# Clamps of converted weights on VectorE in place of GpSimd, and their rounding on ScalarE, in a kernel of attention and two MLPs

## The chip, the cores and the metric

The kernel runs on one core of a Trainium2 chip. A core has five engines that run their own instruction streams side by side: TensorE (PE in the profile, and PEld for its weight loads), VectorE (DVE), ScalarE (ACT), GpSimd (POOL) and SyncE (SP, which here only issues DMAs). The metric is the time of one execution on the device in microseconds, lower is better.

## The reference, cut to what matters

```python
# attention (per batch and head; s = 576 tokens, m = 32 memory rows, d = 64)
a = phi - np.max(phi, axis=2, keepdims=True); a = np.exp(a)
a = a / (np.sum(a, axis=2, keepdims=True) + 1e-09)
k_m = np.einsum('bhsm,bhsd->bhmd', a, k)
v_m = np.einsum('bhsm,bhsd->bhmd', a, v)
scores = scale * np.matmul(q, k_m.transpose(0, 1, 3, 2))
scores = scores - np.max(scores, axis=-1, keepdims=True)
attn = np.exp(scores); attn = attn / (np.sum(attn, axis=-1, keepdims=True) + 1e-09)
x = np.matmul(attn, v_m)            # laid out as 2304 tokens x 512
# first MLP, w_in 512 x 2048, w_out 2048 x 512
h = x @ w_in
x = (h * (1.0 / (1.0 + np.exp(-1.702 * h)))) @ w_out
# norm and second MLP, w_gate and w_val 512 x 1536, w_out 1536 x 512
xn = x / np.sqrt(np.mean(x * x, axis=-1, keepdims=True) + 1e-06) * rms_g
g = xn @ w_gate
out = (g * (1.0 / (1.0 + np.exp(-g))) * (xn @ w_val)) @ w_out
```

The attention's inputs are float32. The five weight matrices come as float64 and are turned into float32 on the chip, by operations on their bits.

## The kernel before, in words

Every float32 product is taken as three passes over TensorE: each operand is split into a high part h (rounded to TensorE's fast 32-bit form) and a low part l, and x y is h h' + l h' + h l'. So each operand of TensorE needs a rounding (h) and a subtraction (l = x - h).

**Staging.** The four batches are worked on as two pairs. For each batch and half of its heads (a unit) the kernel loads k, v, q and phi, takes the softmax of phi, k_m and v_m, and the scores and their softmax. attn @ v_m @ w_in is taken as attn @ (v_m @ w_in), so that v_m @ w_in (vm_part, L422) is a weight of the first MLP. The first MLP runs over 8 blocks of 256 hidden units: a_g1 (L454, then GELU L460 on ScalarE, rounding L462 on ScalarE, low part L109 on GpSimd into gr) and a_g2 (L483), whose results VectorE adds from PSUM into x2 (L491, here called the eviction). a_g2's results go through three PSUM buffers. While pair 0 passes its first MLP, the attention of pair 1 runs beside it as side work. Then pair 1 passes its first MLP, with the RMS norm of pair 0 beside it; the norm of pair 1 (norm_1 to norm_4, L504 to L553) comes in the transition to the second MLP: squares on ScalarE, their sums on GpSimd (L508, L510, low part L109), column sums on TensorE (L521), root and reciprocal (L528, VectorE), transposes (L535). The second MLP (b_g3 at L577, b_g4 at L608) runs over 6 blocks of 256 hidden units.

**The weights' conversion** (w_load and w_conv, from L127). A piece is 128 rows of 512 float64 numbers, 512 KB. It is loaded into one of three raw buffers by SyncE (L133, L135). Then, on the bits: ScalarE takes the absolute value of the upper words into one of three cv buffers (L152); L153 clamps it to the range that float32 holds; VectorE shifts it (L157) and merges in the sign (L161) and the lower word's bits (L164). Pieces of the first MLP are also written to a cache in DRAM from ScalarE's DMA queue (L168), and the second pair loads them from there as float32. At last the high part is rounded by copy(to_h, ...) (L102 where it runs on GpSimd, L106 where on ScalarE) and the low part subtracted (L109, on GpSimd but for one piece). There are 68 conversions: 32 pieces of the first MLP and 36 of the second.

**What sets the order.** A table written by hand gives the first steps, about the first 100 us, and names the engine of some steps; run() gives the rest by rule: after each a_g1 or b_g3 come the conversions due at this place, a load for two pieces ahead, side work, and the a_g2 or b_g4 of the step before. A second table gives the transition. The framework's scheduler then orders each engine's stream by its own estimate of times; an engine executes its stream strictly in this order, and a waiting instruction holds all behind it.

Of the kernel before, what the change touches and what calls it, by code (L numbers as in the profile page):

```python
# [18 lines left out]
def kernel(  # L19
# [43 lines left out]
    MINW = 2.0**-15  # bits 0x38000000  # L63
    MAXW = 122872.0  # bits 0x47EFFC00
# [77 lines left out]
    def w_conv(hf, clamp=G, to_h=G, to_l=G):  # L142
        """float64 to float32, on the bits: sign and top exponent bit, then the other exponent
        bits and the fraction 3 to the left. What is out of float32's range is clamped."""
        raw = loaded.pop(hf)
        if hf[:2] == ("a", 1):
            t = raw[:, :512]
        else:
            bits = raw.rearrange("p (n t) -> p n t", t=2)
            lo, hi = bits[:, :, 0], bits[:, :, 1]  # L150
            t = cvp.tile([P, 512], U32, tag="cv", name="cv")
            nc.scalar.activation(out=t.bitcast(F32), in_=hi.bitcast(F32), func=AF.Abs)  # L152
            clamp.tensor_scalar(  # L153
                out=t.bitcast(F32), in0=t.bitcast(F32), scalar1=MINW, scalar2=MAXW,
                op0=ALU.max, op1=ALU.min,
            )
# [21 lines left out]
    # A unit is four heads of a batch. Where its k and v lay, q^T and the softmax of its scores follow.  # L178
    # The four 32-row blocks of an odd batch hold heads 2, 3, 0, 1.
# [164 lines left out]
    def soft(u, hp):  # L344
        """Of a unit's softmax, blocks 2 hp and 2 hp + 1, by parity and chunk pair; and its sums."""
# [79 lines left out]
        # An odd batch's heads 2, 3, 0, 1 lie in its blocks, so the rows' halves  # L425
        # are of different batches.
# [244 lines left out]
    # Side work of each pass, in the order of its issue.  # L671
# [40 lines left out]
    # Batch 0 first: its share of the first MLP runs beside the rest of batch 1's attention.  # L712
    for s in (
# [24 lines left out]
        (w_conv, w2[1], G, G, V), (a_g1, 0, 1, 1), (w_load, w2[3]), (a_g1, 0, 1, 2),  # L738
# [25 lines left out]
    # The norm of the second pair runs beside the second MLP of the first.  # L764
# [52 lines left out]
```

## Time and profile before

| what | value |
| --- | --- |
| time, median of 3 runs | 922.22 us (921.48 to 923.67) |
| profiled execution, span from first to last instruction | 919.6 us |
| TensorE busy | 866.3 us, 94% |
| VectorE busy | 556.7 us, 61% |
| GpSimd busy | 496.5 us, 54% |
| ScalarE busy | 382.2 us, 42% |

The trace is of one execution, and its only time is the span; the runs of the first line are others. Attention of both pairs and the first MLP of pair 0 last until about 260 us, the first MLP of pair 1 follows until about 440, the transition until about 500, and then the second MLP. The shares are averages over these stages; the rows below take them apart.

### The profile page before, as it was taken

The numbers are of one execution on the slowest core, as the hardware profiler recorded it, in microseconds if no ns is written. First come the engines' busy times: TensorE is split into PE (matmuls) and PEld (weight loads), VectorE is DVE, ScalarE is ACT, GpSimd is POOL, SyncE is SP. The second block draws the span as 40 slices with busy tenths as digits, with TensorE's granted clock in tenths as the row PEclk, the third lists the DMA queues.
The fourth block names the chain that finished last, engine by engine and source line by source line (L and its number), as shares of the span: only waits on it lengthen the run. The fifth ranks groups of instructions, "written<-read, shape, count | busy, mean of one in ns | idle before, by whom it ended". The sixth has DMA issues, their size and how long they took to land.

```text
span 919.6 us, 14798 instructions
## 1 busy us (share of the span) xinstructions
PE 866.3 (94%) x5702; PEld 823.1 (90%) x5702; DVE 556.7 (61%) x997; ACT 382.2 (42%) x823; POOL 496.5 (54%) x450
## 2 busy tenths in 40 slices
PE   3887997997999999999998999999999999999997
PEld 2776997986999999999988999999999999999997
DVE  5699896788965456558778155366348328333333
ACT  2366773654667765554466342122122122111110
POOL 2377998897987695979994162064046018001000
PEclk9989998999999999999999999999999999999999
DMA  9974559433221120223313021012004001000123
GB/s 215 258 218 124 165 137 244 160 118 108 90 70 46 48 69 25 69 73 101 92 47 92 1 92 46 1 46 92 0 1 124 14 1 47 1 1 1 46 58 103
DMA packets 40534, 74.62 MB, mean 81 GB/s; under 512 B 3856, under 2 KB 16144, under 8 KB 40464
## 3 DMA queue, kind: packets, MB, share of 16 engines
q1 hardware_dynamic: 35856, 65.29, 26.2%
q10 hardware_dynamic: 4608, 8.39, 2.6%
q8 instruction: 45, 0.74, 0.3%
q14 instruction: 25, 0.20, 0.1%
HBM read 60.56 MB, written 13.11 MB: 80 GB/s over the span
## 4 chain that ended last, share of the span: by engine, by line
PE 72%; POOL 8%; DVE 7%; DMA 6%; issue 4%; SPq 2%; ACT 1%; ACTq 0%; POOLq 0%; DVEq 0%
PE pg L577 31%; PE pg L608 16%; PE pg L483 14%; PE pg L454 7%; POOL cv L153 2%; DMA stage<-in_k_dram 2%; DVE cv L161 2%; PE pvm L422 2%; DMA raw_a_out<-in_moe_w_out_dram 2%; POOL gr L109 2%; DVE cv L164 1%; DVE x L491 1%; DMA stage<-in_v_dram 1%; DVE cv L157 1%; DMA raw_a_in<-in_moe_w_in_dram 1%
## 5 line engine op out<-in xcount | busy, mean ns | idle before, releaser
L483 PE MATMUL pg<-gr,a_outh 128*128 128x288 f32 x1024 | 231.4, 301 | 11.7 <-DVE x L491 10.2
L483 PEld LDWEIGHTS pg<-gr,a_outh 128*128 128x128 f32 x1024 | 172.8, 190 | 16.4 <-DVE x L491 14.7
L483 PE MATMUL pg<-gr,a_outl 128*128 128x288 f32 x512 | 151.6, 297 | 0.0
L153 POOL TENSOR_SCALAR cv<-cv 128x512 f32<-128x512 f32 x67 | 137.1, 2051 | 22.8 <-ACT cv L152 20.8
L608 PE MATMUL pg<-b_o2h,pp 128*128 128x512 f32 x432 | 139.7, 391 | 0.0
L586 DVE TENSOR_TENSOR pf<-sg,pg 128x384 f32<-128x384 f32 x72 | 39.6, 552 | 158.2 <-PE pg L577 151.0
L109 POOL TENSOR_TENSOR gr<-gf,gr 128x288 fp32r<-128x288 f32 x128 | 115.9, 920 | 34.8 <-ACT gr L462 30.1
L491 DVE TENSOR_TENSOR x<-x,pg 128x288 f32<-128x288 f32 x224 | 95.9, 446 | 61.8 <-PE pg L483 60.7
L102 POOL TENSOR_SCALAR b_o2h<-cv 128x512 fp32r<-128x512 f32 x12 | 8.4, 716 | 223.6 <-PE pg L577 223.4
L584 ACT ACTIVATE sg<-pg 128x384 f32<-128x384 f32 x72 | 35.4, 492 | 159.1 <-PE pg L577 159.0
L483 PEld LDWEIGHTS pg<-gr,a_outl 128*128 128x128 f32 x512 | 97.1, 190 | 0.0
L608 PEld LDWEIGHTS pg<-b_o2h,pp 128*128 128x128 f32 x432 | 81.1, 188 | 16.1
L588 ACT CAST pp<-pf 128x384 fp32r<-128x384 f32 x72 | 37.0, 513 | 126.9 <-DVE pf L586 126.6
L608 PE MATMUL pg<-b_o2l,pp 128*128 128x512 f32 x216 | 84.8, 393 | 0.0
L616 DVE TENSOR_TENSOR oacc<-oacc,pg 128x512 f32<-128x512 f32 x90 | 61.1, 683 | 24.1 <-PE pg L608 24.1
L460 ACT ACTIVATE gf<-pg 128x288 f32<-128x288 f32 x128 | 51.6, 410 | 53.4 <-POOL gr L109 25.2
L109 DVE TENSOR_TENSOR pp<-pf,pp 128x384 fp32r<-128x384 f32 x72 | 46.3, 643 | 34.9 <-ACT pp L588 34.9
L462 ACT CAST gr<-gf 128x288 fp32r<-128x288 f32 x128 | 53.5, 432 | 28.8 <-PE pg L483 25.3
L577 PE MATMUL pg<-xnh,b_gateh 128*128 128x384 f32 x288 | 62.6, 337 | 0.0
L577 PE MATMUL pg<-xnh,b_vall 128*128 128x384 f32 x288 | 62.3, 337 | 0.0
L577 PE MATMUL pg<-xnh,b_gatel 128*128 128x384 f32 x288 | 62.3, 336 | 0.0
L157 DVE TENSOR_SCALAR cv<-cv 128x512 uint32<-128x512 uint32 x68 | 52.0, 765 | 17.0 <-POOL cv L153 16.9
(183 smaller groups left out, 1849.4 us busy)
## 6 DMA issues: line engine op xcount, KB each, us to landing
raw_a_in<-in_moe_w_in_dram SPq DMA_DIRECT2D x16, 512.0 KB, 4.2
raw_a_out<-in_moe_w_out_dram SPq DMA_DIRECT2D x16, 512.0 KB, 4.3
cache<-cv ACTq DMA_DIRECT2D x32, 256.0 KB, 3.8
raw_b_gate<-in_moe_w_gate_dram SPq DMA_DIRECT2D x12, 512.0 KB, 3.7
raw_b_val<-in_moe_w_val_dram SPq DMA_DIRECT2D x12, 512.0 KB, 3.8
raw_b_o<-in_moe_w_out_dram SPq DMA_DIRECT2D x12, 512.0 KB, 3.6
stage<-in_k_dram SPq DMA_DIRECT2D x8, 576.0 KB, 12.1
stage<-in_v_dram SPq DMA_DIRECT2D x8, 576.0 KB, 11.6
```

Source lines behind the costliest of these rows:

```text
L109: eng.tensor_tensor(out=lo, in0=full, in1=hi.bitcast(F32), op=ALU.subtract)
L153: clamp.tensor_scalar(out=t.bitcast(F32), in0=t.bitcast(F32), scalar1=MINW, scalar2=MAXW, op0=ALU.max, op1=ALU.min,)
L157: nc.vector.tensor_scalar(out=t, in0=t, scalar1=3, scalar2=0x3FFFFFFF, op0=ALU.logical_shift_left, op1=ALU.bitwise_and,)
L454: nc.tensor.matmul(ps[:, :HALF], lhsT=a[:, b, c, f], rhs=at[:, y, c, n], start=(i == 0), stop=(i == 5),)
L460: nc.scalar.activation(out=gf[:, :HALF], in_=ps[:, :HALF], func=AF.Gelu_apprx_sigmoid)
L462: nc.scalar.copy(out=gr[:, 0, :HALF], in_=gf[:, :HALF])
L483: nc.tensor.matmul(ps[:, :HALF], lhsT=wo[a][:, fc, es], rhs=gr[fc][:, y, :HALF], start=(i == 0), stop=(i == 5),)
L491: nc.vector.tensor_tensor(out=acc[:, e, n], in0=acc[:, e, n], in1=ps[:, :HALF], op=ALU.add)
L577: nc.tensor.matmul(ps[:, :TB], lhsT=w[a][:, e, f], rhs=xs[y][:, e, n], start=(i == 0), stop=(i == 3 * NE - 1),)
L586: nc.vector.tensor_tensor(out=pf, in0=sg, in1=pss[1][:, :TB], op=ALU.mult)
L608: nc.tensor.matmul(ps, lhsT=pp[fc][:, a, ks], rhs=w[y][:, fc], start=(i == 0), stop=(i == 5))
L616: nc.vector.tensor_tensor(out=o, in0=o, in1=ps, op=ALU.add)
```

## The change

The clamp (L153) of every converted piece is issued on VectorE. Before, one of the 68 ran there and 67 on GpSimd. The rounding of the high part of every converted piece is issued on ScalarE; before, 6 of these ran there and 62 on GpSimd. GpSimd keeps the rounding of pieces that the second pair loads from the cache, and the low parts. Comments are emptied too; the line numbers stay. The diff's core, with three of the six changed lines of the table:

```diff
-    def w_conv(hf, clamp=G, to_h=G, to_l=G):
+    def w_conv(hf, to_h=None, to_l=G):
...
             nc.scalar.activation(out=t.bitcast(F32), in_=hi.bitcast(F32), func=AF.Abs)
-            clamp.tensor_scalar(
+            nc.vector.tensor_scalar(
                 out=t.bitcast(F32), in0=t.bitcast(F32), scalar1=MINW, scalar2=MAXW,
                 op0=ALU.max, op1=ALU.min,
             )
...
         x, (h, l) = t.bitcast(F32), wt[key]
-        copy(to_h, h[:, c], x)
+        copy(to_h or (G if hf[:2] == ("a", 1) else A), h[:, c], x)
         sub_lo(to_l, l[:, c], x, h[:, c])
...
-        (att_k5, b0), (att_k5, b1), (w_load, w0[3]), (w_conv, w0[1], G, A), (vm_part, 0, 0, 0),
+        (att_k5, b0), (att_k5, b1), (w_load, w0[3]), (w_conv, w0[1]), (vm_part, 0, 0, 0),
...
-        (w_conv, w1[1], G, A), (w_conv, w2[0], V, A), (a_g2, 0, 0, 0), (aside,),
+        (w_conv, w1[1]), (w_conv, w2[0]), (a_g2, 0, 0, 0), (aside,),
...
-        (w_conv, w2[1], G, G, V), (a_g1, 0, 1, 1), (w_load, w2[3]), (a_g1, 0, 1, 2),
+        (w_conv, w2[1], A, V), (a_g1, 0, 1, 1), (w_load, w2[3]), (a_g1, 0, 1, 2),
```

The scheduler orders the streams anew. Three places follow. Numbers behind a name tell instances apart (cv_2153 is one piece's conversion, gr_1879 one GELU's parts), and what stands in brackets is what the instruction waits for.

On ScalarE, before, where the attention of the third unit (kmisc2_1) runs beside the first MLP's fourth block; gf and gr are GELU and its rounding:

```order
L462 CAST gr_1790<-gf_1788 128x288 [waits PE_49,Activation_49]
L168 DMA cache_102<-cv_1969 128x512 [waits DMAHW5_49,DVE_49]
L460 ACTIVATE gf_1865<-pg1_1858 128x288 [waits Pool_49]
L462 CAST gr_1867<-gf_1865 128x288 [waits PE_49,Activation_49]
L245 ACT_TABLE_LOAD [waits DMAHW7_49]
L245 ACTIVATE kmisc2_1_1440<-kmisc2_1_1440 96x768 [waits Pool_49]
L460 ACT_TABLE_LOAD
L460 ACTIVATE gf_1877<-pg1_1870 128x288 [waits Pool_49]
L462 CAST gr_1879<-gf_1877 128x288 [waits PE_49,Activation_49]
```

The cache write of cv_1969 waits for DMA semaphore 5; the roundings gr_1867 and gr_1879 follow with no Abs between them.

On ScalarE, after, the same cache write, and then the stretch up to gr_1879:

```order
L168 DMA cache_102<-cv_1969 128x512 [waits DMAHW4_49,DVE_49]
L460 ACTIVATE gf_1865<-pg1_1858 128x288 [waits Pool_49]
L106 CAST a_0_4_outh_1976<-cv_1969 128x512
L242 COPY kmisc2_1_1440<-pk3_1616 96x128 [waits PE_49]
L168 DMA cache_102<-cv_2074 128x512 [waits DMAHW6_49,DVE_49]
L460 ACTIVATE gf_1877<-pg1_1870 128x288 [waits Pool_49]
L106 CAST a_0_4_outh_1976<-cv_2074 128x512
```

```order
L462 CAST gr_1867<-gf_1865 128x288 [waits PE_49,Activation_49]
L460 ACT_TABLE_LOAD
L460 ACTIVATE gf_1952<-pg1_1945 128x288 [waits Pool_49]
L460 ACTIVATE gf_1964<-pg1_1957 128x288 [waits Pool_49]
L152 ACTIVATE cv_2153<-raw_a_0_5_in_0_1980 128x512 [waits DMAHW3_49,DMAHW2_49]
L297 ACTIVATE kz_1720<-pk4_1689,rv_1716 128x64 [waits DVE_49,PE_49]
L302 ACTIVATE vz_1724<-pk4_1689,rv_1716 128x64 x2
L462 CAST gr_1879<-gf_1877 128x288 [waits PE_49]
L433 CAST vm0_4h_1982<-pvm_1984 64x2x256 [waits PE_49]
```

The write of cv_1969 waits for DMA semaphore 4 now, roundings of weights (L106) have come between the GELUs, and the Abs of cv_2153 has moved up, ahead of gr_1879. That Abs waits for its piece's load.

On VectorE, before, the evictions of the same block (pg2):

```order
L491 TENSOR_TENSOR x2_0_822<-x2_0_822,pg2_1753 128x288
L491 TENSOR_TENSOR x2_0_822<-x2_0_822,pg2_1761 128x288
L491 TENSOR_TENSOR x2_0_822<-x2_0_822,pg2_1826 128x288
L491 TENSOR_TENSOR x2_0_822<-x2_0_822,pg2_1834 128x288
L491 TENSOR_TENSOR x2_0_822<-x2_0_822,pg2_1842 128x288
L251 TENSOR_REDUCE kmisc2_1_1440<-kmisc2_1_1440 96x128
L491 TENSOR_TENSOR x2_0_822<-x2_0_822,pg2_1850 128x288
```

On VectorE, after, from pg2_1826 on:

```order
L491 TENSOR_TENSOR x2_0_822<-x2_0_822,pg2_1826 128x288
L491 TENSOR_TENSOR x2_0_822<-x2_0_822,pg2_1834 128x288
L287 TENSOR_SCALAR rv_1716<-pk4s_1714 128x1
L290 RECIPROCAL rv_1716<-rv_1716 128x1
L291 TENSOR_SCALAR rv_1716<-maskeo_99,rv_1716 128x3
L491 TENSOR_TENSOR x2_0_822<-x2_0_822,pg2_1842 128x288
L153 TENSOR_SCALAR cv_2153<-cv_2153 128x512
L491 TENSOR_TENSOR x2_0_822<-x2_0_822,pg2_1850 128x288
L157 TENSOR_SCALAR cv_2153<-cv_2153 128x512
L161 SCALAR_TENSOR_TENSOR cv_2153<-raw_a_0_5_in_0_1980,cv_2153 128x512
```

Here too cv_2153 has moved up: its clamp and its shift stand on either side of pg2_1850.

On GpSimd, before, in the transition, the norm of pair 1 (sq and sr are squares and their sums) and pieces of the second MLP's second block (b_1):

```order
L508 TENSOR_TENSOR sq0_1_0_5895<-sq0_1_0_5895,sq1_1_0_5896 128x768
L153 TENSOR_SCALAR cv_6341<-cv_6341 128x512
L510 TENSOR_TENSOR sq0_1_0_5895<-sq0_1_0_5895 128x384
L109 TENSOR_TENSOR sr_5901<-sq0_1_0_5895,sr_5901 128x384
L508 TENSOR_TENSOR sq0_1_1_6004<-sq0_1_1_6004,sq1_1_1_6005 128x768
L102 TENSOR_SCALAR b_1_gateh_6019<-cv_6013 128x512
L102 TENSOR_SCALAR b_1_gateh_6019<-cv_6267 128x512
L510 TENSOR_TENSOR sq0_1_1_6004<-sq0_1_1_6004 128x384
L109 TENSOR_TENSOR b_1_gatel_6020<-cv_6013,b_1_gateh_6019 128x512
L109 TENSOR_TENSOR b_1_gatel_6020<-cv_6267,b_1_gateh_6019 128x512
L153 TENSOR_SCALAR cv_6535<-cv_6535 128x512
L109 TENSOR_TENSOR sr_6010<-sq0_1_1_6004,sr_6010 128x384
```

On GpSimd, after, the same place:

```order
L508 TENSOR_TENSOR sq0_1_0_5895<-sq0_1_0_5895,sq1_1_0_5896 128x768
L510 TENSOR_TENSOR sq0_1_0_5895<-sq0_1_0_5895 128x384
L109 TENSOR_TENSOR sr_5901<-sq0_1_0_5895,sr_5901 128x384
L508 TENSOR_TENSOR sq0_1_1_6004<-sq0_1_1_6004,sq1_1_1_6005 128x768
L510 TENSOR_TENSOR sq0_1_1_6004<-sq0_1_1_6004 128x384
L109 TENSOR_TENSOR b_1_gatel_6020<-cv_6013,b_1_gateh_6019 128x512
L109 TENSOR_TENSOR b_1_gatel_6020<-cv_6267,b_1_gateh_6019 128x512
L109 TENSOR_TENSOR sr_6010<-sq0_1_1_6004,sr_6010 128x384
L508 TENSOR_TENSOR sq0_1_2_6023<-sq0_1_2_6023,sq1_1_2_6024 128x768
L510 TENSOR_TENSOR sq0_1_2_6023<-sq0_1_2_6023 128x384
L109 TENSOR_TENSOR sr_6029<-sq0_1_2_6023,sr_6029 128x384
L109 TENSOR_TENSOR b_1_vall_6348<-cv_6341,b_1_valh_6347 128x512
```

The clamps and the roundings between the norm's sums are gone; the sums and the low parts stay in their order.

## Rows read from the trace of the kernel before

**Rows 1.** The page: span, busy time, TensorE's busy tenths in 40 slices.

```profile
span 919.6 us, 14798 instructions
...
PE 866.3 (94%) x5702; PEld 823.1 (90%) x5702; DVE 556.7 (61%) x997; ACT 382.2 (42%) x823; POOL 496.5 (54%) x450
...
PE   3887997997999999999998999999999999999997
```

**Rows 2.** Busy by stage: length, five engines, granted clock, DMA share, GB/s.

```profile
40.00:100.00 60.00, 47.13 (x385) 42.84 (x385) 54.06 (x110) 39.54 (x97) 44.87 (x37) 0.94 0.61 177
100.00:180.00 80.00, 72.50 (x571) 69.73 (x569) 61.42 (x114) 47.61 (x111) 69.81 (x64) 0.96 0.65 172
180.00:260.00 80.00, 71.93 (x582) 69.54 (x583) 70.87 (x132) 45.94 (x102) 73.98 (x66) 0.98 0.36 115
300.00:440.00 140.00, 139.83 (x1067) 139.28 (x1067) 87.41 (x174) 83.11 (x193) 115.05 (x119) 1.00 0.23 67
440.00:500.00 60.00, 55.82 (x337) 53.30 (x336) 47.95 (x77) 36.90 (x65) 49.40 (x37) 0.97 0.23 68
500.00:920.00 420.00, 414.92 (x2190) 388.98 (x2188) 190.66 (x298) 90.90 (x172) 100.59 (x75) 1.00 0.13 39
80.00:100.00 20.00, 15.14 (x149) 14.04 (x150) 18.93 (x34) 13.79 (x34) 17.06 (x14) 1.00 0.37 120
```

**Rows 3.** TensorE's waits, 40 to 260: line, what it waited for, total, times, longest.

```profile
PE pg L483 <- DVE x L491: 9.5, 8, 5.2
PE pg L454 <- ACT gf L460: 4.0, 1, 4.0
...
PE pq L397 <- POOL stage L385: 1.5, 2, 1.1
```

**Rows 4.** TensorE's waits, 440 to 500.

```profile
PE pnr L535 <- DVE r L528: 3.4, 1, 3.4
```

**Rows 5.** The chain of waits, 440 to 500, by line.

```profile
by line: PE pg L577 17.8%; POOL cv L153 14.1%; issue 9.2%; POOL sq L508 9.1%; POOL gr L109 6.2%; POOL sr L109 6.1%; POOL sq L510 5.6%; PE pg L483 4.4%; POOL b_gatel L109 4.2%; PE pg L608 3.5%; PE pg L454 3.1%; POOL b_valh L102 3.0%; ACT sq 
```

**Rows 6.** Groups by line, 40 to 260: count, busy us, mean ns, idle before.

```profile
L153 POOL TENSOR_SCALAR cv<-cv 128x512 f32<-128x512 f32 x29 | 59.9, 2067 | 7.9 <-ACT cv L152 7.1
L157 DVE TENSOR_SCALAR cv<-cv 128x512 uint32<-128x512 uint32 x30 | 21.6, 720 | 2.7 <-POOL cv L153 2.6
```

**Rows 7.** Line L153 by engine: shortest, median, longest ns; first and last start.

```profile
L153 DVE TENSOR_SCALAR cv<-cv x1: 826/826/826, 82.4 to 82.4; 128x512 f32<-128x512 f32 x1
```

**Rows 8.** Busy by stage of line L157 alone: length, VectorE, clock, DMA, GB/s.

```profile
40.00:100.00 60.00, 5.15 (x9) 0.94 0.61 177
100.00:180.00 80.00, 8.57 (x11) 0.96 0.65 172
180.00:260.00 80.00, 7.89 (x10) 0.98 0.36 115
440.00:500.00 60.00, 7.08 (x8) 0.97 0.23 68
```

**Rows 9.** Line L157: shortest, median, longest ns.

```profile
L157 DVE TENSOR_SCALAR cv<-cv x68: 357/794/1515, 34.1 to 780.3; 128x512 uint32<-128x512 uint32 x68
```

**Rows 10.** Timelines of VectorE and GpSimd near 214: start, us, instruction.

```profile
213.88 5.53 DVE L161 SCALAR_TENSOR_TENSOR cv<-raw_a_out,cv 128x512 uint32<-128x512 uint32 x1
...
213.54 2.02 POOL L244 TENSOR_TENSOR kmisc<-kmisc 96x768 f32<-96x768 f32 x1
```

**Rows 11.** Line L106, the roundings of one weight on ScalarE.

```profile
L106 ACT CAST a_inh<-cv x4: 610/622/633, 45.5 to 86.9; 128x512 fp32r<-128x512 f32 x4
```

**Rows 12.** Timeline of ScalarE near 157; in brackets idle before, and releaser.

```profile
157.06 0.41 ACT L460 ACTIVATE gf<-pg 128x288 f32<-128x288 f32 x1 [7.65 <-DMA stage<-in_k_dram]
```

**Rows 13.** Timeline of SyncE near 150, the loads' issue.

```profile
150.15 2.97 SPq L135 DMA_DIRECT2D raw_a_in<-in_moe_w_in_dram  x2
```

**Rows 14.** DMA issues, 125 to 165: count, KB each, median us to landing.

```profile
raw_a_in<-in_moe_w_in_dram SPq DMA_DIRECT2D x3, 512.0 KB, 13.7
```

**Rows 15.** Timeline of VectorE near 161.

```profile
161.55 0.43 DVE L491 TENSOR_TENSOR x<-x,pg 128x288 f32<-128x288 f32 x1
```

More of the change, by code (lines that the diff above doesn't have):

```diff
@@ L724 @@
         (att_q3, a1, 0), (att_q3, a1, 1), (att_q3s, a1, 1, G), (att_k4, b1), (att_q3s, a1, 0, G),
-        (att_k5, b0), (att_k5, b1), (w_load, w0[3]), (w_conv, w0[1], G, A), (vm_part, 0, 0, 0),
+        (att_k5, b0), (att_k5, b1), (w_load, w0[3]), (w_conv, w0[1]), (vm_part, 0, 0, 0),
         (vm_part, 0, 0, 1), (att_q4, a0, 0), (att_q4, a1, 1), (att_q4, a0, 1), (w_conv, w0[2]),
-        (att_q4, a1, 0), (narrow,), (att_q1, b1, 1), (w_conv, w0[3], G, A), (w_load, w1[0]),
-        (att_q1, b0, 0), (w_load, w1[1]), (w_conv, w1[0], G, A), (att_q1, b1, 0), (att_q3, b1, 1),
+        (att_q4, a1, 0), (narrow,), (att_q1, b1, 1), (w_conv, w0[3]), (w_load, w1[0]),
+        (att_q1, b0, 0), (w_load, w1[1]), (w_conv, w1[0]), (att_q1, b1, 0), (att_q3, b1, 1),
         (att_q3, b1, 0), (aside,), (att_q1, b0, 1, V), (att_q3s, b1, 1, V), (aside,),
@@ L731 @@
         (att_q3, b0, 0), (aside,), (w_load, w1[3]), (att_q4, b1, 0), (att_q3s, b0, 1, G),
-        (att_q3s, b0, 0, V), (att_q4, b0, 0), (att_q4, b0, 1), (w_conv, w1[2], G, A),
+        (att_q3s, b0, 0, V), (att_q4, b0, 0), (att_q4, b0, 1), (w_conv, w1[2]),
         (att_q4, b1, 1), (w_load, w2[0]), (a_g1, 0, 0, 1), (a_g1, 0, 0, 2), (a_g2, 0, 0, 1),
-        (w_conv, w1[1], G, A), (w_conv, w2[0], V, A), (a_g2, 0, 0, 0), (aside,),
+        (w_conv, w1[1]), (w_conv, w2[0]), (a_g2, 0, 0, 0), (aside,),
         (vm_next, 0, 1, 0), (aside,), (vm_next, 0, 1, 1), (w_load, w2[1]), (a_g1, 0, 0, 3),
```

## The prediction, made before the changed kernel ran

> **What bounds the kernel now.** I read the page first, then the busy time by stage, then in each stage what ended the waits. The page gives TensorE 94% busy in a span of 919.6 us, and its row of slices (23 us each) shows where the missing time lies: the first four slices, and the 7th, 10th and 22nd [rows 1]. The table by stage says it in numbers [rows 2]. From 300 to 440 us TensorE is busy 139.83 of 140 us, from 500 to 920 us 414.92 of 420, and what is missing there is the tail after the last matmul. Nothing that GpSimd, VectorE or ScalarE does in these 560 us can gain anything. The open time is 12.9 us idle in 40 to 100, 7.5 in 100 to 180, 8.1 in 180 to 260 and 4.2 in 440 to 500: 32.7 us in all. To it comes the lowered clock that a long pause leaves behind: 0.97 in 440 to 500 is 1.8 us of 60. The change can gain no more than a part of these.
>
> In 40 to 260 both GpSimd and VectorE are nearly full. GpSimd has 44.87 + 69.81 + 73.98 = 188.7 of 220 us, VectorE 54.06 + 61.42 + 70.87 = 186.4 [rows 2]. Which of the two TensorE waits for is told by its list of waits [rows 3]: 9.5 us in 8 waits for VectorE's evictions (L491), 4.0 once for a GELU on ScalarE (L460), and for GpSimd itself 1.5. In 440 to 500 it is different: the one long wait is 3.4 us for the norm's reciprocal on VectorE (L528) [rows 4], and the chain there runs mostly over GpSimd, L153 alone with 14.1% of it [rows 5].
>
> **What the change moves, and its price.** GpSimd loses all its clamps. In 40 to 260 these are 29 of 2067 ns, 59.9 us [rows 6]: its load falls from 188.7 to 128.8 us, and the 25 roundings that also leave it there make it less still. It stops being nearly full.
>
> VectorE gains the clamps. One clamp already ran there, beside a busy GpSimd, in 826 ns [rows 7]. Its nearest kin is L157, of the same shape, type width and place, which took 5.15 us for 9 in 40 to 100 (0.57 each), 8.57 for 11 in 100 to 180 (0.78), 7.89 for 10 in 180 to 260 (0.79) and 7.08 for 8 in 440 to 500 (0.89) [rows 8]. The ends I keep are the shortest and the longest L157, 0.357 and 1.515 us [rows 9]. I take L157's mean in each stage, since the clamp will stand a place or two ahead of L157 in the same traffic. So VectorE gets 9 x 0.57 = 5.1 us in 40 to 100, 11 x 0.78 = 8.6 in 100 to 180, 10 x 0.79 = 7.9 in 180 to 260 and 8 x 0.89 = 7.1 in 440 to 500.
>
> The longest VectorE instruction of the attention stage is no clamp and no L157 but an L161, 5.53 us, and it ran beside a two-input GpSimd instruction (L244) [rows 10]; L157 spreads from 0.357 to 1.515 us for one and the same work [rows 9]. The Trainium skill ("Advanced Engine Details and Errata", section VectorE Performance Modes) says that VectorE's second SBUF port is shared with GpSimd, and that instructions using both ports and GpSimd's instructions block each other. The trace agrees in part: there is such a spread, but the means of 0.57 to 0.89 lie well inside it, so no row bears out that every instruction is blocked. What the rule would make of this change is a rival below.
>
> ScalarE gains the 25 roundings in 40 to 260. Four like them already ran there, 0.62 us each [rows 11]: 15.5 us on 39.54 + 47.61 + 45.94 = 133.1 of 220 [rows 2]. I cost that at nothing. What hides it is ScalarE's idle 87 us; if it were not hidden, each would delay one GELU by 0.62 us. In 500 to 920 ScalarE has 90.90 of 420 and VectorE 190.66, so the clamps and roundings there, and those before 40 us and from 260 to 440, cost nothing while TensorE stays fed: at most 2 us, kept for the range.
>
> Now the stages. The densest row of VectorE has 18.93 of 20 us, 94.7% [rows 2]; I take this as the fullest that it gets.
> - 40 to 100: 54.06 + 5.1 = 59.2 us, which at 94.7% needs 62.5. **+2.5 us**.
> - 100 to 180: 61.42 + 8.6 = 70.0 of 80, not full. The long wait here is not GpSimd's: ScalarE sat 7.65 us at a cache write (L168), until a semaphore of one of nine stage loads, and TensorE waited 4.0 us of that for the GELU behind it [rows 3, 12]. In the new order that write waits for an earlier load, but the Abs of the next group's first weight (cv_2153) now stands ahead of gr_1879 on ScalarE, and its clamp ahead of evictions on VectorE. That weight lands about 150.15 + 13.7 = 163.9 us [rows 13, 14], later than the evictions beside it would come without the old stall. I put one wait for the other: **0**.
> - 180 to 260: 70.87 + 7.9 = 78.8 us of 80. TensorE's longest wait, 5.2 us, is the L161 of 5.53 us beside GpSimd [rows 3, 10]. With 10 x 2.07 = 20.7 us of clamps gone, GpSimd has 53 of 80 us and pauses, so I take that L161 out, down to a plain L157's 0.79: 78.8 - 4.7 = 74.1 us, at 94.7% 78.2. **-1.8 us**.
> - 440 to 500: VectorE 47.95 + 7.1 = 55.0, below 94.7% of 60. GpSimd's chain loses 8 clamps, and the norm's sums come up to that much sooner. The 3.4 us wait goes, and with it the lowered clock behind it, 1.8: **-5 us** of the 4.2 + 1.8 there are.
> - Short waits of VectorE for GpSimd's clamps in 40 to 260: L157 waited 2.6 us [rows 6]. **-1 us**.
>
> The sum is 2.5 + 0 - 1.8 - 5 - 1 = -5.3 us. On the profiled execution: 919.6 - 5.3 = 914.3 us of span. The median of the runs shown is 922.22, so 2.6 us lie outside this execution's span or are scatter; I carry them along: **917 us**.
>
> What is queued behind the new waits: behind each clamp on VectorE stand evictions (L491), for which TensorE waits, since three accumulator buffers are all it has; behind each rounding on ScalarE a GELU or its rounding (L460, L462). A late weight used to hold GpSimd, now it holds these.
>
> **The rivals.**
> *A. VectorE has room after all.* The clamps come at 0.357 us, and the wait at the cache write goes without a successor. For it: the write's load is an earlier one of the nine, and GpSimd is silent more often. Against it: GpSimd's two-input work is all still there. 40 to 100 becomes (54.06 + 9 x 0.357) / 0.947 = 60.5, so +0.5 in place of +2.5; the 4.0 us at the cache write are gained, and 1.8 of lowered clock as in 440 to 500. 917 - 2.0 - 5.8 = 909 us, and with some of the short waits for L491 907.
> *B. VectorE becomes the bound (slower).* Clamps at 0.826 us, and the long L161 comes again, since what stood beside it was a two-input instruction, not a clamp. (54.06 + 9 x 0.826) / 0.947 = 64.9, +4.9; (70.87 + 10 x 0.826) / 0.947 = 83.6, +3.6; the norm gains 2 in place of 5, as its own VectorE steps queue behind clamps. 4.9 + 3.6 - 2 = +6.5: 929 us. It decides as soon as VectorE's load in both stretches passes 94.7% of what they last. For it: evictions already are the longest list of waits. Against it: VectorE idles 18.6 us in 100 to 180.
> *C. The late weight costs more than the write did.* The eviction behind the stall came at 161.55 [rows 15], and without the 4.0 us the next would come about 157.5; the weight is through Abs and clamp at about 165.5 (two instructions of 0.8 behind 163.9). 8 us less the 4.0 that the old wait took is +4, and up to 5 with the clock: -5.3 + 5, about 922 us, no change.
> *D. Port by the rule.* If all 29 clamps wait as the longest L157, 186.4 + 29 x 1.515 = 230.3 us in 40 to 260, at 94.7% 243.2, +23.2; with the norm's -5: about 940 us. The means in [rows 8] speak against it. This is what the Trainium skill's sentence on the shared port would give.
>
> **How the numbers follow.** Forecast 0.43 (its own range 912 to 922), A 0.20, B 0.22, C 0.10, D 0.05. The range runs from 903, a little below A, to 932, a little above B, and leaves D and the ends out. A measurement of this kernel tells 0.2%, about 1.8 us, from no change: 920.4 to 924.1 is the same. Faster: A, and 0.34 of the forecast's, some of C: 0.55. Same: 0.07 of the forecast's and 0.06 of C: 0.13. Slower: B, D and the rest: 0.32.
>
> **What would show it.** Right: VectorE's busy share in 40 to 100 and 180 to 260 at about 94%, clamps on it at 0.6 to 0.9 us, no VectorE instruction over 3 us from 200 to 230, no 3 us wait for L528, 300 to 440 and the second MLP unchanged. Wrong: longer waits for L491 than 9.5 us (B), a TensorE wait of over 5 us beside the nine loads with ScalarE at L152 (C), clamps at 0.36 (A) or above 1.2 us (D), or any TensorE idle in the second MLP, which no case here has.

## The result, and the profile after

The changed kernel is slower: 928.89 us median (923.91 to 931.15, 9 runs) against 921.62 for the kernel before (918.53 to 923.67, 9 runs). The ratio is 1.0074 with a 95% interval of 1.0054 to 1.0095, about 7 us. The prediction said 917. The profiled execution of after has a span of 923.9 us, 4.3 over that of before, and a run's time is 1.8 us above its span (923.91 to 922.1 in the quickest run). Executions of one kernel lie up to 12 us apart (917.03 to 928.62 for the kernel before in one group of runs), and the traced execution of after (925.67) is one of its quicker ones, so its trace holds 4.3 of the 7 us. Below, single traces are read by stretches and whole kernels by medians.

First the page of after: span, busy time, and TensorE's slices, against [rows 1].

```profile
span 923.9 us, 14790 instructions
...
PE 865.8 (94%) x5702; PEld 822.9 (89%) x5702; DVE 551.5 (60%) x1064; ACT 412.3 (45%) x885; POOL 321.2 (35%) x321
...
PE   4866889979999999999997999999999999999997
```

VectorE took 67 more clamps and is busy 5 us less than before; GpSimd lost 175 us. TensorE is below nine tenths in slices 1 to 6, 9, 22 and the last; before, slices 5 and 6 were full. By stage, with the columns of [rows 2]:

```profile
40.00:100.00 60.00, 42.54 (x345) 38.70 (x343) 47.69 (x106) 39.36 (x91) 24.41 (x24) 0.83 0.59 170
100.00:180.00 80.00, 73.16 (x589) 70.09 (x589) 67.44 (x134) 53.85 (x129) 41.03 (x43) 1.00 0.66 183
180.00:260.00 80.00, 72.92 (x587) 70.18 (x586) 66.36 (x140) 50.53 (x111) 45.33 (x46) 0.98 0.34 110
440.00:500.00 60.00, 54.25 (x339) 52.58 (x338) 44.15 (x83) 37.67 (x65) 29.03 (x22) 0.94 0.23 72
```

From 40 to 100 TensorE is busy 42.54 us in place of 47.13, and at a clock of 0.83 in place of 0.94. In the same stretch VectorE fell from 54.06 to 47.69: the stage got slower with every engine less busy, which is the mark of waits and not of load. TensorE's waits there, 40 to 260, against [rows 3], and 440 to 500, against [rows 4]:

```profile
PE pg L454 <- ACT gf L460: 6.7, 4, 2.8
PE pq L397 <- DVE stage L385: 5.6, 1, 5.6
PE pg L483 <- DVE x L491: 5.3, 7, 2.2
PE pg L483 <- ACT gr L462: 3.8, 1, 3.8
```

```profile
PE pg L577 <- ACT sg L584: 5.0, 1, 5.0
PE pnr L535 <- DVE r L528: 0.7, 1, 0.7
```

One more line of the list of before, 40 to 260, is needed, which [rows 3] left out:

```profile
PE pq L397 <- DVE stage L385: 2.7, 1, 2.7
```

The evictions (L491) are no longer first, and the norm's reciprocal has gone from 3.4 to 0.7. One wait has doubled: 5.6 us in place of 2.7 for the normalisation of the scores of pair 0's last attention unit (L385). Two are new: 3.8 us for a GELU's rounding (L462) and 5.0 for a sigmoid (L584). Each is a place in an engine's stream.

**The 5.6 us.** VectorE's timeline of before from the last score sum (L378) to L385:

```profile
77.32 0.55 DVE L378 TENSOR_REDUCE stage<-stage 96x12 f32<-96x384 f32 x1 [0.46 <-ACT stage L374]
77.96 0.46 DVE L109 TENSOR_TENSOR attnT<-pq,attnT 128x288 fp32r<-128x288 f32 x1
78.33 2.50 DVE L381 TENSOR_SCALAR stage<-stage 96x12 f32<-96x12 f32 x1
80.86 0.22 DVE L384 RECIPROCAL stage<-stage 96x12 f32<-96x12 f32 x1
81.12 1.32 DVE L385 TENSOR_TENSOR stage<-stage 96x384 f32<-96x384 f32 x1
82.36 0.83 DVE L153 TENSOR_SCALAR cv<-cv 128x512 f32<-128x512 f32 x1
```

and of after:

```profile
80.98 0.69 DVE L153 TENSOR_SCALAR cv<-cv 128x512 f32<-128x512 f32 x1 [0.72 <-ACT cv L152]
81.60 0.54 DVE L378 TENSOR_REDUCE stage<-stage 96x12 f32<-96x384 f32 x1
82.06 0.59 DVE L157 TENSOR_SCALAR cv<-cv 128x512 uint32<-128x512 uint32 x1
82.57 1.77 DVE L381 TENSOR_SCALAR stage<-stage 96x12 f32<-96x12 f32 x1
84.26 0.68 DVE L161 SCALAR_TENSOR_TENSOR cv<-raw_a_in,cv 128x512 uint32<-128x512 uint32 x1
84.86 0.41 DVE L153 TENSOR_SCALAR cv<-cv 128x512 f32<-128x512 f32 x1
...
85.64 0.67 DVE L164 SCALAR_TENSOR_TENSOR cv<-raw_a_in,cv 128x512 uint32<-128x512 uint32 x1
86.24 0.41 DVE L157 TENSOR_SCALAR cv<-cv 128x512 uint32<-128x512 uint32 x1
86.58 0.54 DVE L385 TENSOR_TENSOR stage<-stage 96x384 f32<-96x384 f32 x1
```

Before, the first clamp came behind L385. Now six steps of two pieces' conversions stand between the unit's scores (its last L373) and L385 (0.69 + 0.59 + 0.68 + 0.41 + 0.67 + 0.41 = 3.45 us), and the first of them waited 0.72 for its Abs. TensorE, whose next instruction is the transpose (L397), begins to wait at 81.7 us. Of its 5.6 us the five later steps fill 2.8 us, which is about what the wait has grown by (2.9). The rest is the unit's own steps, with an L381 that took 1.77 us (2.50 before).

**The 3.8 us.** The exponential of the scores (L374) and the GELU (L460) need different tables on ScalarE. Its timeline of before:

```profile
66.02 1.28 ACT L460 ACT_TABLE_LOAD   x1
...
69.88 0.41 ACT L460 ACTIVATE gf<-pg 128x288 f32<-128x288 f32 x1
70.77 1.28 ACT L374 ACT_TABLE_LOAD   x1
```

and of after:

```profile
64.03 1.28 ACT L460 ACT_TABLE_LOAD   x1
65.32 0.71 ACT L460 ACTIVATE gf<-pg 128x288 f32<-128x288 f32 x2
66.05 1.28 ACT L374 ACT_TABLE_LOAD   x1
67.34 0.52 ACT L374 ACTIVATE stage<-stage 96x384 f32<-96x384 f32 x1
67.78 0.41 ACT L462 CAST gr<-gf 128x288 fp32r<-128x288 f32 x1
68.21 1.28 ACT L460 ACT_TABLE_LOAD   x1
69.50 0.41 ACT L460 ACTIVATE gf<-pg 128x288 f32<-128x288 f32 x1
```

Before, six of pair 0's eight exponentials stood ahead of the first GELU, and the other two behind this group of four GELUs and their roundings. Now the sixth stands behind the second GELU, and two more table loads of 1.28 us stand ahead of the rounding for which TensorE waits from 66.9 to 70.7. The Trainium skill ("ScalarE: Activation LUTs", section What ACT_TABLE_LOAD costs) gives 1283 ns for the load, which the rows show, and about 1380 ns more for a drain at each switch to another set; these rows show no such pause (64.03 + 1.28 is 65.31, the GELU starts at 65.32, and the load before it starts 0.02 after the exponential).

**The 5.0 us.** ScalarE's timeline of after in the transition:

```profile
488.26 0.68 ACT L152 ACTIVATE cv<-raw_b_gate 128x512 f32<-128x512 f32 x1 [1.61 <-DMA raw_b_gate<-in_moe_w_gate_dram]
488.96 1.28 ACT L584 ACT_TABLE_LOAD   x1
490.25 0.49 ACT L584 ACTIVATE sg<-pg 128x384 f32<-128x384 f32 x1
```

The Abs of a piece whose load was issued at 484.5 stands ahead of the sigmoid and waits for the load. Before, the sigmoid ran at 484.33 and this Abs behind it:

```profile
484.33 0.49 ACT L584 ACTIVATE sg<-pg 128x384 f32<-128x384 f32 x1
...
489.50 0.67 ACT L152 ACTIVATE cv<-raw_b_gate 128x512 f32<-128x512 f32 x1
```

In all three a step that TensorE does not need now stands ahead of a short one that it waits for: conversions twice, an exponential with its table loads once. That the scheduler moved them up because the long clamp no longer holds the conversions back is not shown; e2 below keeps the long clamps and loses too. ScalarE's waits for raw weights, 40 to 260, were 4.6 us in 4 waits before (4.2 + 0.4) and are 16.7 us in 7 after (9.1 + 7.6).

### The profile page after: what moved, and what is told of

Read it like the earlier page. It is cut to its first block, busy times and chain, and to the rows that moved or that the text cites. A ratio compares the mean times of both kernels' runs of the same rounds, so it can differ in the third digit from the quotient of the medians.

```text
span 923.9 us, 14790 instructions
## 1 busy us (share of the span) xinstructions
PE 865.8 (94%) x5702; PEld 822.9 (89%) x5702; DVE 551.5 (60%) x1064; ACT 412.3 (45%) x885; POOL 321.2 (35%) x321
## 4 chain that ended last, share of the span: by engine, by line
PE 77%; DVE 9%; DMA 5%; ACT 5%; issue 3%; SPq 1%; POOL 0%; ACTq 0%; DVEq 0%
PE pg L577 32%; PE pg L483 17%; PE pg L608 16%; PE pg L454 8%; PE pvm L422 2%; DMA raw_a_in<-in_moe_w_in_dram 2%; DMA raw_a_out<-in_moe_w_out_dram 2%; DVE cv L164 1%; DVE cv L153 1%; DVE cv L161 1%; DVE x L491 1%; DMA stage<-in_v_dram 1%; DVE cv L157 1%; PE pq L360 1%; ACT L460 1%
## 5 line engine op out<-in xcount | busy, mean ns | idle before, releaser
L483 PE MATMUL pg<-gr,a_outh 128*128 128x288 f32 x1024 | 234.0, 300 | 10.4 <-DVE x L491 6.5
L483 PEld LDWEIGHTS pg<-gr,a_outh 128*128 128x128 f32 x1024 | 173.4, 189 | 14.2 <-DVE x L491 9.5
L483 PE MATMUL pg<-gr,a_outl 128*128 128x288 f32 x512 | 151.6, 297 | 0.0
L109 POOL TENSOR_TENSOR gr<-gf,gr 128x288 fp32r<-128x288 f32 x128 | 112.6, 892 | 101.2 <-ACT gr L462 97.9
L608 PE MATMUL pg<-b_o2h,pp 128*128 128x512 f32 x432 | 140.3, 391 | 0.0
L491 DVE TENSOR_TENSOR x<-x,pg 128x288 f32<-128x288 f32 x224 | 97.4, 448 | 63.4 <-PE pg L483 62.4
L109 POOL TENSOR_TENSOR b_o2l<-cv,b_o2h 128x512 fp32r<-128x512 f32 x12 | 15.3, 1295 | 257.9 <-PE pg L577 203.2
L483 PEld LDWEIGHTS pg<-gr,a_outl 128*128 128x128 f32 x512 | 97.0, 190 | 0.0
L584 ACT ACTIVATE sg<-pg 128x384 f32<-128x384 f32 x72 | 35.2, 489 | 136.5 <-PE pg L577 136.4
L608 PEld LDWEIGHTS pg<-b_o2h,pp 128*128 128x128 f32 x432 | 81.1, 188 | 15.9
L608 PE MATMUL pg<-b_o2l,pp 128*128 128x512 f32 x216 | 84.6, 392 | 0.0
L460 ACT ACTIVATE gf<-pg 128x288 f32<-128x288 f32 x128 | 51.3, 412 | 44.8 <-POOL gr L109 24.9
L577 PE MATMUL pg<-xnh,b_valh 128*128 128x384 f32 x288 | 62.7, 338 | 5.0 <-ACT sg L584 5.0
L577 PE MATMUL pg<-xnh,b_vall 128*128 128x384 f32 x288 | 62.5, 337 | 0.0
L577 PE MATMUL pg<-xnh,b_gatel 128*128 128x384 f32 x288 | 62.3, 336 | 0.0
L577 PE MATMUL pg<-xnl,b_gateh 128*128 128x384 f32 x288 | 62.2, 334 | 0.0
L577 PE MATMUL pg<-xnh,b_gateh 128*128 128x384 f32 x288 | 62.0, 336 | 0.0
L577 PE MATMUL pg<-xnl,b_valh 128*128 128x384 f32 x288 | 61.8, 336 | 0.0
L109 DVE TENSOR_TENSOR pp<-pf,pp 128x384 fp32r<-128x384 f32 x72 | 39.9, 556 | 32.6 <-ACT pp L588 32.6
```

Of the source, the lines that this page charges most:

```text
L109: eng.tensor_tensor(out=lo, in0=full, in1=hi.bitcast(F32), op=ALU.subtract)
L460: nc.scalar.activation(out=gf[:, :HALF], in_=ps[:, :HALF], func=AF.Gelu_apprx_sigmoid)
L483: nc.tensor.matmul(ps[:, :HALF], lhsT=wo[a][:, fc, es], rhs=gr[fc][:, y, :HALF], start=(i == 0), stop=(i == 5),)
L491: nc.vector.tensor_tensor(out=acc[:, e, n], in0=acc[:, e, n], in1=ps[:, :HALF], op=ALU.add)
L577: nc.tensor.matmul(ps[:, :TB], lhsT=w[a][:, e, f], rhs=xs[y][:, e, n], start=(i == 0), stop=(i == 3 * NE - 1),)
L584: nc.scalar.activation(out=sg, in_=pss[0][:, :TB], func=AF.Silu)
```

## The experiments

Theories: the order (above); the load, that VectorE has too much to do (rival B); and ScalarE's roundings. The kernels are the changed kernel with the engines chosen by piece, and with what else is named:

```diff
-            nc.vector.tensor_scalar(
+            clamp_on(hf).tensor_scalar(
...
-        copy(to_h or (G if hf[:2] == ("a", 1) else A), h[:, c], x)
+        copy(round_on(hf), h[:, c], x)
```

The diffs below show what clamp_on and round_on return; in the changed kernel that is V and A, and G for the rounding of cached pieces throughout. "old" is the engine that the kernel before had for the piece. Ratios are to the kernel before, which ran beside each group of runs (medians 923.5, 920.2, 921.0 and 921.7); they are not quite the quotients of the medians.

| run | median us | ratio, 95% interval |
| --- | --- | --- |
| e3 start only | 930.93 | 1.0066, 1.0046 to 1.0086 |
| e4 middle only | 928.11 | 1.0048, 1.0023 to 1.0074 |
| e5 second MLP only | 925.47 | 1.0022, 1.0000 to 1.0044 |
| e1 clamps only | 926.48 | 1.0032, 1.0007 to 1.0056 |
| e2 roundings only | 929.99 | 1.0099, 1.0063 to 1.0135 |
| e6 start, four clamps back | 917.93 | 0.9964, 0.9939 to 0.9988 |
| e7 second MLP, one line later | 924.09 | 1.0032, 1.0006 to 1.0057 |
| e8 no clamps at all | 920.49 | 0.9993, 0.9967 to 1.0018 |
| f1 all, four clamps back | 920.37 | 0.9980, 0.9955 to 1.0006 |
| f2 start, clamps only | 923.42 | 1.0017, 0.9991 to 1.0044 |
| f3 middle, writes from GpSimd | 922.80 | 1.0007, 0.9983 to 1.0030 |
| h1 start, two late clamps back | 935.78 | 1.0146, 1.0105 to 1.0187 |
| h2 start, two early clamps back | 925.18 | 1.0017, 0.9990 to 1.0043 |
| h3 e6, writes from GpSimd | 927.71 | 1.0061, 1.0036 to 1.0085 |
| h4 h3 and the middle | 924.14 | 1.0020, 0.9995 to 1.0045 |

The traces are read in stretches between named matmuls, in us. Start: 1st to 97th of L454. Middle: to the 577th of L483. Rest: to the 625th of L454. Transition: to the 577th of L577. From there to the last of L608 all take 303.1. What comes ahead of the start is left out: it is 57.9 us in before and 59.5 in after, but it scatters (57.7 in e6, 66.2 in h3, whose VectorE has the same order there).

| trace | start | middle | rest | transition |
| --- | --- | --- | --- | --- |
| before | 54.6 | 133.8 | 140.2 | 225.0 |
| after | 63.0 | 128.2 | 137.4 | 227.3 |
| e3 | 63.4 | 129.7 | 140.9 | 225.1 |
| h1 | 57.6 | 130.6 | 153.6 | 226.3 |
| h2 | 60.0 | 129.0 | 138.3 | 226.5 |
| e6 | 55.3 | 124.8 | 140.7 | 225.8 |
| e4 | 55.2 | 141.1 | 137.4 | 224.9 |
| f3 | 55.3 | 135.6 | 137.8 | 226.6 |
| e5 | 54.5 | 134.8 | 140.2 | 228.5 |
| e7 | 55.1 | 132.9 | 140.2 | 227.3 |
| e8 | 64.7 | 124.5 | 137.2 | 226.2 |
| e1 | 60.5 | 128.4 | 137.3 | 226.6 |
| e2 | 58.8 | 137.1 | 136.3 | 228.6 |
| f1 | 56.2 | 129.8 | 137.8 | 227.7 |
| f2 | 57.1 | 128.3 | 142.4 | 226.0 |
| h3 | 55.5 | 133.5 | 142.2 | 226.3 |
| h4 | 56.9 | 132.4 | 137.9 | 226.6 |

Where an edit does not touch a stretch or what comes ahead of it, the traces show what is scatter: 54.5 to 55.3 in the start (before, e4, f3, e5, e7), 132.9 to 134.8 in the middle (before, e5, e7). In the transition, kernels that leave the second MLP as it was have 224.9 to 226.6.

**By stage: e3, e4, e5.**

```diff
# e3
+        return V if hf[0] == "a" and hf[2] < 3 else old       # clamp_on
+        return A if hf[0] == "a" and hf[2] < 3 else old       # round_on
# e4
+        return V if hf[0] == "a" and hf[2] >= 3 else old      # clamp_on
+        return A if hf[0] == "a" and hf[2] >= 3 else old      # round_on
# e5
+        return V if hf[0] == "b" else old                     # clamp_on
+        return A if hf[0] == "b" else old                     # round_on
```

Expected of e3: 

> Change only in the first MLP's blocks 0 to 2 of pair 0 (12 pieces, about the first 140 us), everything else as before. Theory 1 (the loss is made in the start, where ScalarE's and VectorE's streams put conversions ahead of the attention's steps): TensorE is 6 to 9 us late at 95 us as in the changed kernel, and most of it stays: +4 to +8 us, about 927. Theory 2 (the start's delay is absorbed by slack of the rest of the pair, and the loss that counts is made in the transition to the second MLP): within 2 us of before, about 922. Theory 3 (VectorE's mere load is too high from 40 to 260): half of the loss, +3 to +4.

Expected of e4: 

> Change only in the first MLP's blocks 3 to 7 of pair 0 (20 pieces, about 140 to 280 us). Theory 1: the 5.5 us L161 and the 7.7 us wait at the cache write go or shrink, and nothing else is lost: -3 to -6 us, about 917. Theory 2: likewise -3 to -6. Theory 3 (VectorE's load): +3 to +4.

Expected of e5: 

> Change only in the second MLP's pieces (36, from about 430 us on). Theory 2: the Abs of a piece whose load comes late stands ahead of a sigmoid on ScalarE, TensorE waits 5 us at L577 as in the changed kernel, where before it waited 3.4 us for L528: +2 to +4 us, about 925. Theory 1: within 1 us of before, since one wait takes the other's place.

The start alone costs 8.8 us in its stretch (63.4 against 54.6), as in after (63.0), with the same two waits of 5.6 and 3.8. The second MLP alone costs 3.5 in the transition. On the middle theories 1 and 2 were wrong: it loses 7.3 us in its stretch, and its time (+0.48%) is about what theory 3, the load, had said; f3 below decides between them. The parts do not add: 0.66 + 0.48 + 0.22 = 1.36% against 0.74% for all. Where the start is edited, the middle is quicker, in e3 too, where the middle is unchanged (129.7 against 133.8). That is not the start's delay coming back: e6 below has hardly any delay (55.3) and a middle that is quicker still (124.8).

**The middle: f3.** The trace of e4 has on ScalarE, as [rows 12] of before, a cache write (L168) that stands until a stage load lands:

```profile
159.84 0.33 ACTq L168 DMA_DIRECT2D cache<-cv  x1
160.22 0.41 ACT L460 ACTIVATE gf<-pg 128x288 f32<-128x288 f32 x1 [8.02 <-DMA stage<-in_k_dram]
```

```diff
-                nc.scalar.dma_start(out=cached(hf), in_=t.bitcast(F32))
+                (nc.gpsimd if hf[2] > 2 else nc.scalar).dma_start(out=cached(hf), in_=t.bitcast(F32))
```

Expected: 

> The change in blocks 3 to 7 of pair 0 alone (+0.48%), with these blocks' cache writes issued from GpSimd in place of ScalarE. If the 8.0 us that ScalarE stands at a cache write until a stage load lands is what holds the middle: the 5.7 us wait of TensorE for the GELU behind it goes, and the clock behind it, 6 to 8 us less, at 921 less 1 to 4. If the late loads themselves hold it (the next step needs them anyway): no change, +4 us over before.

The 8.0 us wait is gone from ScalarE's list, the 5.7 us wait of TensorE behind it too, and the middle takes 135.6 in place of 141.1; the time falls from +0.48% to +0.07%, with all clamps of the middle still on VectorE, where the load theory would keep +3 to +4 us. Some of it comes back: ScalarE's Abs now wait 11.9 us in 4 waits for these writes, which hold the cv buffers. In after the same write goes at 157.73 without a wait for a load; ScalarE reaches it some 8 us later than before (157.06 - 7.65 = 149.41), with the loads landed. But this is not all that makes a middle quick: f1's ScalarE still waits 6.4 us there, and its middle takes 129.8. What else does is open.

**Clamps or roundings: e1, e2.**

```diff
# e1
+        return V         # clamp_on
+        return old       # round_on
# e2
+        return old       # clamp_on
+        return A         # round_on
```

Expected of e1: 

> All clamps on VectorE, the roundings as before (6 on ScalarE, 62 on GpSimd). If VectorE's new load is what costs: as the changed kernel, +6 to +8 us, about 929. If ScalarE's roundings in front of GELUs and sigmoids cost: at before or below, 915 to 922.

Expected of e2: 

> All roundings of converted pieces on ScalarE, the clamps as before (67 on GpSimd, 1 on VectorE). If the clamps on VectorE are the larger half of the loss (they alone gave +0.32%): within 3 us of before. If the roundings are, or if any new order costs: +4 to +6 us.

Neither half is harmless. e1 lies between its two expectations, e2 above both of its own, and the half without the clamps on VectorE is the slower: 1.0099 for the roundings. So VectorE's load is not needed for a loss. That it plays no part is not shown by these two.

**No clamps: e8.** The four lines of the clamp are left out.

Expected: 

> The changed kernel with all 68 clamps left out (what lies outside float32's range is not clamped). If VectorE's 68 clamps are the loss by their duration: 7 us or more below the changed kernel, at or under before. If the loss is in the order in which loads, Abs and the rest stand: still 3 us or more over before, since VectorE waits at the same places.

The time is at before's, some 0.8% below the changed kernel, as the load theory had said; by the time alone that theory would stand. For the start the trace decides against it. With no clamp on any engine, TensorE's wait for L385 is longer than with them, and the start takes 64.7 us:

```profile
PE pq L397 <- DVE stage L385: 8.7, 1, 8.7
```

So in the start it is not the clamps' time that costs. What e8 gains over after lies in the middle (124.5 against 128.2) and the transition (226.2 against 227.3, within the scatter); whether the clamps' time or the order makes the middle's gain is open.

**The start's two places: e6, h1, h2.** Four clamps on GpSimd (three of them as before; that of block 2 in 0 ran on VectorE) take the conversions out from before L385 and put six exponentials ahead of the first GELU again; two of them do only the one, two only the other.

```diff
# e6: BACK = block 0 in 1, block 0 out 0, block 1 out 1, block 2 in 0
# h1: BACK = block 1 out 1, block 2 in 0      h2: BACK = block 0 in 1, block 0 out 0
+        return G if hf in BACK else V if hf[0] == "a" and hf[2] < 3 else old   # clamp_on
```

VectorE's order in h1 and e6 has no conversion between the last L373 and L385 of this unit (six in the changed kernel), in h2 three. ScalarE's order in e6 and h2 has six exponentials ahead of the first GELU, in h1, as in the changed kernel, five. In e6 and h2 one exponential still stands among the GELUs, behind the third (in e6 with table loads at 68.29 and 70.45), so the edit moves the table loads by one GELU and does not remove them.

Expected of e6: 

> The change in blocks 0 to 2 of pair 0 alone, as in the run of +0.66%, but the clamps of four of its twelve pieces on GpSimd again. By that, the conversions leave the gap between the last score sums (L373) and the normalisation (L385) on VectorE, and the exponentials stand ahead of all first GELUs on ScalarE. Order theory (those two places are the loss): the 5.6 us wait for L385 and the 3.8 us wait for L462 shrink to below 3 and below 1 us, and the time comes within 2 us of before. Load theory (VectorE has too much to do): a third of the loss goes, 4 us over before.

Expected of h1: 

> The change in blocks 0 to 2 of pair 0 alone (+0.66%), with two late clamps on GpSimd again (block 1: out 1; block 2: in 0): no conversion stands between L373 and L385 on VectorE, but one exponential still stands among the GELUs on ScalarE. If the conversions before L385 are the larger place: 4 to 7 us off, +0 to +2 us over before. If the table swaps on ScalarE are: 1 to 3 us off.

Expected of h2: 

> As the run before this one, but with two early clamps on GpSimd again (block 0: in 1 and out 0): all exponentials ahead of the first GELUs, but three conversion steps still between L373 and L385. If the table swaps on ScalarE are the larger place: 4 to 7 us off the +0.66%; if the conversions before L385 are: 1 to 3 us off.

In the start's stretch the parts nearly add: h1 takes 5.8 us off e3, h2 3.4, both (e6) 8.1. TensorE's longest waits from 40 to 110, in e6:

```profile
PE pg L483 <- ACT x L106: 2.1, 1, 2.1
...
PE pg L483 <- ACT gr L462: 0.9, 2, 0.5
```

In h1 the wait for L385 is 1.7 us and that for L462 still 3.4. Both waits are as the order theory had said for e6 (below 3 and below 1 us) in e6's trace, though table loads still stand among its GELUs. VectorE's load in 40 to 100 does not tell a quick start from a slow one. It is high in two quick ones (54.90 of 60 us in e6, 54.06 in before) and low in two slow ones (47.69 in after, 48.50 in e3), but lower still in h1 (46.84), whose start is quicker than e3's. Nor does the clock granted in the start's stretch: e5 has 0.87 and is quick (54.5), h2 has 1.00 and is not (60.0). The whole times do not follow the stretch. h1 is 1.46% over before where 0 to 2 us had been expected, since its rest takes 153.6 us in place of 140.9, in steps that the edit doesn't touch: TensorE idles 1.9 us from 280 to 290 and 3.9 from 300 to 310, and its clock is 0.81 and 0.85 from 280 to 300, where e3 has no idle time and the full clock. The scheduler rewrites the order there too; which step of it costs this I have not followed. By the whole times, h2 (0.49 points off e3) would make the GELUs the larger place and h1 no place at all, against the stretches. So a median of one such kernel is no verdict on the place that was edited.

**All with four back: f1; without roundings: f2.** f1 is the changed kernel with e6's four pieces back; f2 is e6 with all roundings old.

Expected of f1: 

> The changed kernel with the clamps of four pieces (block 0: in 1, out 0; block 1: out 1; block 2: in 0) on GpSimd again; the other 64 on VectorE, all roundings on ScalarE. If the start's order is most of the change's loss: 7 to 9 us below the changed kernel, at before's level or just under. If the middle (+0.48% alone) and the second MLP (+0.22%) keep their losses when the start is mended: +4 to +6 us over before.

Expected of f2: 

> As the run that was 0.36% below before (eight of the first twelve clamps on VectorE), but all roundings as before. If the gain there comes from the clamps that left GpSimd: again 2 to 4 us below before. If it comes from the roundings: at before.

Four of 68 clamps move the whole change from 1.0074 to 0.9980, that is 0.94% or 8.7 us; with the start's order mended, the change's loss is gone, though 64 clamps are still on VectorE. In the traces the start is the stretch that gains (56.2 against 63.0; no other is shorter than in after). e6's gain over before lies in the middle (124.8 against 133.8), and it does not come from the clamps alone (f2 is at before).

**The transition: e7.**

```diff
-        (norm_4, 1, 0, 1), (norm_4, 1, 0, 2), (norm_4, 1, 0, 3), (norm_1, 1, 1), (w_conv, h1[0]),
+        (norm_4, 1, 0, 1), (norm_4, 1, 0, 2), (norm_4, 1, 0, 3), (norm_1, 1, 1),
...
-        (norm_1, 1, 2), (norm_2, 1, 1), (norm_3, 1, 1), (norm_4, 1, 1, 0), (b_g3, 0, 1),
+        (norm_1, 1, 2), (norm_2, 1, 1), (norm_3, 1, 1), (norm_4, 1, 1, 0), (b_g3, 0, 1), (w_conv, h1[0]),
```

Expected: 

> The change in the second MLP's pieces alone, as in the run of +0.22%, with one line of the second table moved: w_conv of h1[0] five steps later, by which the Abs of the late piece (b, 2, gate, 0) comes to stand behind the sigmoid sg of the third block of columns. Order theory: the 5.1 us wait at L577 goes, and the norm's gain shows: 3 to 5 us below before's level. Load theory: no change against that run, 2 us over before.

The late Abs now stands behind the sigmoid, and the wait at L577 falls from 5.1 to 2.9 us, but that for L528 rises from 0.7 to 1.7, and the stretch only goes from 228.5 to 227.3, which is within the scatter; the medians show no gain. That is what the load theory had said of e7, and the order theory's 3 to 5 us below before did not come. The trace shows the late Abs as one cause of the wait at L577; that it costs the kernel time is not shown.

**Towards a better version: h3, h4.** e6, and e6 with the middle, each with the cache writes of blocks 3 to 7 from GpSimd.

Expected of h3: 

> The version that was 0.36% below before (change in blocks 0 to 2, four clamps on GpSimd), with the cache writes of blocks 3 to 7 issued from GpSimd. That version's trace shows no wait of ScalarE at a cache write any more, so that little is left to gain: 0 to 2 us below it, 3 to 5 below before. If GpSimd's own queue delays its low parts instead: 2 us above it.

Expected of h4: 

> As the run before this one, and the change in blocks 3 to 7 too; the second MLP as before. Start mended (-0.36% alone), middle with its writes from GpSimd (+0.07% alone): 2 to 5 us below before if the parts add.

Both miss. e6 has no wait at a cache write for a stage load left to mend, and h3's middle takes 133.5 us in place of e6's 124.8. e6 stays the one version that beats both kernels, by 0.36% over before; it is the best of fifteen and was run on one occasion, so that some of the 0.36% may be luck.

## Why the prediction was wrong

- **The step that failed is "40 to 100: +2.5 us"**, worked out as VectorE's load over the fullest share it reaches. The stretch lost 8.4 us with VectorE at 79%. What came in place of a full VectorE is waits: TensorE idles 14.5 us of the start's stretch where it idled 8.1 before, which is 6.4 of the 8.4; the clock there is 0.89 in place of 0.94. The list behind [rows 3] had the wait for L385, at 2.7 us the third longest, and I passed over it. Nor did I read the order of the streams there: I read it at the cache write and in the norm, not around L385 and the first GELUs, though it shows the six conversion steps ahead of L385 and the exponential among the GELUs.
- **"440 to 500: -5 us"** failed too. The 3.4 us wait for L528 shrank to 0.7 as said, but 5.0 us at the sigmoid took its place: the transition is 2.3 us longer (0.7 above the scatter), and the clock in 440 to 500 fell from 0.97 to 0.94 where it should have risen. This is rival C's mechanism, a late weight at the head of ScalarE, at a place where I did not look for it.
- **"100 to 180: 0" and "180 to 260: -1.8"** were too small: the middle stretch gave 5.6 us. The wait at the cache write went, and the 5.53 us L161 of [rows 10] did not come again. f3 shows that the write held the middle of e4. Why the middle of after is quicker is open: e6 with hardly a delay in the start is quicker still, and f1 has the wait and a quick middle. The rest, which the sum had at nothing, is 2.8 us shorter, also without a cause found.
- **The price of the clamp** was a little high and did not decide. By stage, VectorE's clamps of after:

```profile
40.00:100.00 60.00, 4.05 (x9) 0.83 0.59 170
100.00:180.00 80.00, 8.87 (x12) 1.00 0.66 183
180.00:260.00 80.00, 5.63 (x9) 0.98 0.34 110
440.00:500.00 60.00, 3.71 (x7) 0.94 0.23 72
```

That is 0.45 to 0.74 us each, where [rows 8] gave 0.57 to 0.89.
- **ScalarE's roundings "at nothing"** was wrong as a rule: e2 is 1.0099. They took 0.62 us as in [rows 11], so no price of theirs was wrong; ScalarE's idle time did not hide the new order that came with them.
- **Rival B** gave 929 us, the measured time, but not by its mechanism, so the number is luck. It needs VectorE above 94.7% in 40 to 100 and 180 to 260, and after has 79% and 83%; f1 loses nothing with 64 of the 68 clamps on VectorE, and e8's start is slow without any. Only e8's whole time speaks for it. Rival D, the port: by the Trainium skill ("Advanced Engine Details and Errata", section VectorE Performance Modes) GpSimd and those VectorE instructions that use both ports block each other; VectorE's busy time fell from 556.7 to 551.5 us as GpSimd's fell by 175, so the trace agrees with the rule's direction, but here it makes for a gain, as GpSimd lost more work than VectorE got.

## What to carry to other kernels

Where a scheduler orders the streams, an edit of a step's engine or length is an edit of the order: compare the order of each waiting engine around each stretch that already loses time, and ask which steps have come up ahead of those on TensorE's path. Judge such an edit by the stretch between two named matmuls, since the rest of the program is reordered too. For the same reason the parts of a change need not add, and a quicker stretch behind a slower one need not be the delay coming back: look for a kernel that has the one without the other, as e6 here.

## What was not expected of the hardware

L157 on VectorE fell from a median of 794 ns [rows 9] to 420 in after, the same instruction on the same tile:

```profile
L157 DVE TENSOR_SCALAR cv<-cv x68: 396/420/1405, 30.7 to 781.2; 128x512 uint32<-128x512 uint32 x68
```

It is 428 ns in e2, which has the clamps on GpSimd still, and 419 in e1, which has the roundings there. But the median jumps, since the durations lie in two groups. By the times in the traces, an L157 with no GpSimd instruction beside it has a median of 416 to 422 ns in all four kernels, and one that runs mostly beside a low part (L109) on GpSimd 1027 in before, 1024 in e2, 914 in e1 and 664 in after. What changed is how many run alone: 9 of 68 in before, 20 in e2, 36 in e1, 40 in after. The clamp itself, a mean of 2067 ns on GpSimd from 40 to 260 [rows 6], has a median of 426 ns and a mean of 599 on VectorE in after: more than three to one by the means, for one input and the same tile.
